# A recurrent memory-attention branch rebuilt around token-stationary column tiles, a list-scheduled order and precomputed tokens

One core of a Trainium2 chip (trn2). The metric is the device time of one execution in microseconds (us).

## The reference, cut to what matters

```python
# A: sliding-window attention over 2048 tokens, D = 640, 32 heads of 20, window 256
# B: 64 segments of 32 tokens, one after the other; 32 heads of 192; 8 memory tokens
mem = mem0
for s in range(64):
    h = concat([mem, x[:, 32*s : 32*s+32]])          # 40 tokens
    q, k, v = h @ Wq, h @ Wk, h @ Wv                 # each 640 x 6144
    p = softmax(where(mask, q k^T * 192**-0.5, -1e9))
    o = (p v) @ Wo                                   # 6144 x 640
    mem = o[:, :8]                                   # the next segment needs this
    outs.append(o[:, 8:])
out = g * A + (1 - g) * B                            # g = sigmoid(x . gate_w)
```

The recurrence makes B a chain of 64 steps. Its four weights are 31.5 MB; both kernels keep a part of them on the chip and load the rest anew in every step.

One caution for all that follows: with these inputs A is of order 1 and B of order 0.001 (its weights carry factors of 640^-0.5 and 6144^-0.5, A's do not). The comparison with the reference hardly sees B.

## The kernel before

```python
def stage_QK(s, g, hT, b, which):                 # 4 groups of 8 heads per step
    ps = ps_mm.tile([P, 512], FP32, name="ps_proj", tag="mm")
    for j in range(TG):                           # 12 column tiles of 128
        for kt in range(KT):                      # 5: D = 5 x 128
            nc.tensor.matmul(ps[:, j*L:(j+1)*L], lhsT=w_tile(which, kt, t), rhs=hT[:, kt, :], ...)   # L = 40
    ...
def stage_V_units(s, g, b, hT):                   # per pair of heads, both of 192
    wvt = wst.tile([P, 1920], BF, name="wv_chunk", tag="w")          # a ring of 5
    nc.sync.dma_start(wvt[:], WvR[i])                                # Wv is streamed whole
    for kt in range(KT):
        nc.tensor.matmul(ps[0:L, ...],    lhsT=hT[:, kt, :], rhs=wv[:, kt, 0:192],   tile_position=(0, 0))
        nc.tensor.matmul(ps[64:64+L, ...], lhsT=hT[:, kt, :], rhs=wv[:, kt, 192:384], tile_position=(0, 64))
...
for k in range(-1, NG + 2):                       # order made by hand: projections of k+1, v of k, output of k-2
    ...
ov = o_ps[:, 0:KT*L]
hT_next = new_hT(s + 1)                           # five small loads, issued late
nc.vector.tensor_copy(hT_next[:, :, 0:M], ov[:, :, 0:M])
```

Wq and Wk are resident, Wv is streamed (16 units of 480 KB per step), Wo in part (4 units).

## Time and profile before

| | before |
|---|---|
| time, median of 2 runs | 3121.92 us (3118.11 to 3125.73) |
| span of the profiled run | 3116.1 us |
| branch A, then the wait for weights | to about 562, to 590 us |
| one step of B | 39.36 us, 64 steps 2519 us |
| array's own work in a step (worked out in the prediction) | 32 us |

Two answers. (The array is TensorE, called PE in the profile; DVE, ACT and POOL are VectorE, ScalarE and GpSimd; "x63" counts instructions.) The first is the view by instruction, cut to one: the cast of the 8 memory tokens into the next step's input, which ends each step; its first and last start give the step, (3067.3 - 626.8)/62. The second is a window of 1600 us inside the loop: busy time of PE, weight load, DVE, ACT, POOL, then granted clock, DMA share and GB/s.

```profile
L587 DVE CAST hT<-ps_o x63: 198/200/201, 626.8 to 3067.3; 128x40 bf16<-128x40 f32 x63
```

```profile
900.00:2500.00 1600.00, 1444.71 (x41309) 1263.49 (x41307) 861.36 (x2037) 438.36 (x1018) 149.27 (x283) 0.98 0.77 257
```

The array is busy 90% of the time.

### The profile page before, as it was taken

What the parts mean: (1) busy time and instruction counts of PE and PEld (TensorE: products, weight loads), DVE (VectorE), ACT (ScalarE), POOL (GpSimd) and SP (SyncE); (2) the same over time, 40 slices, a digit from 0 to 9 for tenths busy, and PEclk for the clock granted to TensorE, in tenths of its full rate; (3) what the DMA queues carried; (4) which work ended last, traced back from release to release, by engine and by line L of the source; (5) the groups of instructions that cost most, each with busy time, mean ns of one, the idle gap of its engine ahead of it and who ended that gap; (6) DMA issues with size and microseconds to landing.
All of it is one profiled execution on the core that took longest, in us unless ns stands there. A gap on an engine that the chain in (4) does not pass through costs nothing.

```text
span 3116.1 us, 155848 instructions
## 1 busy us (share of the span) xinstructions
PE 2739.6 (88%) x71941; PEld 2385.6 (77%) x71957; DVE 1752.1 (56%) x4221; ACT 1102.7 (35%) x2561; POOL 332.2 (11%) x625
## 2 busy tenths in 40 slices
PE   6888888589888889889989999999999998998898
PEld 5777777478777777777777777777788777777777
DVE  5777777355555555555555555555555555555554
ACT  5778787222222222222222222222222222222222
POOL 4300100001000000000000000000000000000000
PEclk9899899799999999999999999999999999999999
DMA  7600000777777777777777777777777777777776
GB/s 256 232 15 15 21 13 8 269 243 265 249 260 250 249 250 257 258 253 254 260 246 257 260 259 259 259 259 262 258 268 261 257 258 250 252 259 253 246 260 219
DMA packets 224367, 699.56 MB, mean 225 GB/s; under 512 B 35416, under 2 KB 50528, under 8 KB 223072
## 3 DMA queue, kind: packets, MB, share of 16 engines
q1 hardware_dynamic: 200624, 646.79, 61.5%
q0 software_dynamic: 22432, 41.98, 4.2%
q8 instruction: 562, 9.21, 1.2%
q10 hardware_dynamic: 656, 0.82, 0.1%
q14 instruction: 93, 0.76, 0.1%
HBM read 671.76 MB, written 17.70 MB: 221 GB/s over the span
## 4 chain that ended last, share of the span: by engine, by line
PE 48%; DVE 19%; DMA 12%; ACT 12%; issue 8%; POOL 1%; SPq 1%; another core or an unknown queue 0%; ACTq 0%; POOLq 0%; DVEq 0%
PE ps_proj L414 14%; DMA wv_chunk<-WvR 9%; PE ps_v L477 8%; PE ps_o L521 7%; PE S_ps L433 4%; ACT a_ex L194 3%; PE PT_ps L457 3%; PE ps_pv L496 3%; DVE sm_sum L449 3%; DVE sm_mx L444 3%; ACT sm_ex L447 3%; ACT a_pt L204 2%; ACT OTg L500 2%; DVE Vp L482 2%; DVE Pg_12543 L452 2%
## 5 line engine op out<-in xcount | busy, mean ns | idle before, releaser
L477 PE MATMUL ps_v<-wv_chunk,hT 128*40 128x192 bf16 x5120 | 615.0, 252 | 61.2 <-DMA wv_chunk<-WvR 58.2
L479 PE MATMUL ps_v<-wv_chunk,hT 128*40 128x192 bf16 x5120 | 616.2, 252 | 2.0 <-issue 2.0
L414 PE MATMUL ps_proj<-hT,Wq_sb 128*128 128x40 bf16 x15360 | 468.0, 181 | 61.1 <-issue 42.2
L414 PEld LDWEIGHTS <-Wq_sb 128*128 128x128 bf16 x15360 | 433.4, 96 | 89.2 <-issue 82.8
L477 PEld LDWEIGHTS <-hT 128*40 128x40 bf16 x5120 | 396.2, 100 | 58.0 <-issue 24.3
L521 PE MATMUL ps_o<-OTg,Wo_res 128*128 128x40 bf16 x11520 | 405.4, 181 | 16.7 <-issue 3.4
L479 PEld LDWEIGHTS <-hT 128*40 128x40 bf16 x5120 | 384.3, 100 | 43.5 <-issue 38.8
L521 PEld LDWEIGHTS <-Wo_res 128*128 128x128 bf16 x11520 | 357.2, 97 | 77.8 <-issue 68.5
L397 POOL DMA_DIRECT2D hT<-xT_dram x320 | 172.2, 545 | 2006.4 <-PE ps_v L479 1966.4
L484 ACT CAST Vp<-ps_v 40x384 bf16<-40x384 f32 x512 | 242.8, 474 | 386.0 <-DVE Vp L482 377.8
L482 DVE CAST Vp<-ps_v 40x384 bf16<-40x384 f32 x512 | 277.8, 543 | 100.6 <-PE ps_v L479 98.6
L194 ACT ACTIVATE a_ex<-s_ps,a_nmx 128x384 bf16<-128x384 f32 (+2 forms) x512 | 289.2, 613 | 75.3 <-DVE a_nmx L192 74.8
L192 DVE TENSOR_REDUCE a_nmx<-s_ps 128x1 f32<-128x384 f32 (+2 forms) x512 | 254.2, 524 | 28.9 <-PE s_ps L189 21.2
L502 DVE CAST OTg<-ps_pv 128x240 bf16<-128x240 f32 x256 | 104.4, 408 | 272.6 <-PE ps_pv L496 272.6
L414 PE MATMUL ps_proj<-hT,Wk_a 128*128 128x40 bf16 x7680 | 235.6, 182 | 20.3 <-issue 20.0
L414 PEld LDWEIGHTS <-Wk_a 128*128 128x128 bf16 x7680 | 217.5, 97 | 32.9 <-issue 32.6
L414 PE MATMUL ps_proj<-hT,Wk_b 128*128 128x40 bf16 x7680 | 236.5, 180 | 5.0 <-issue 4.0
L414 PEld LDWEIGHTS <-Wk_b 128*128 128x128 bf16 x7680 | 216.7, 96 | 16.0 <-issue 15.9
L500 ACT CAST OTg<-ps_pv 128x240 bf16<-128x240 f32 x256 | 91.9, 359 | 353.5 <-PE ps_pv L496 352.0
L420 DVE CAST KTg_12536<-ps_proj 128x480 bf16<-128x480 f32 x128 | 84.2, 658 | 222.8 <-PE ps_proj L414 222.8
L201 PE MATMUL pt_ps<-a_ident,a_ex 128*128 128x128 bf16 x1440 | 161.7, 220 | 42.0 <-ACT a_pt L204 27.4
L449 DVE TENSOR_REDUCE sm_sum<-sm_ex 40x8 f32<-40x320 f32 x256 | 122.3, 478 | 117.3 <-ACT sm_ex L447 113.4
(1165 smaller groups left out, 4481.1 us busy)
## 6 DMA issues: line engine op xcount, KB each, us to landing
wv_chunk<-WvR SPq DMA_DIRECT2D x1024, 480.0 KB, 4.9
wo_chunk<-WoR SPq DMA_DIRECT2D x256, 480.0 KB, 5.2
Wq_sb<-in_B_Wq_dram POOLq DMA_DIRECT2D x5, 1536.0 KB, 13.0
rp_t<-in_B_Wv_dram POOLq DMA_DIRECT2D x16, 480.0 KB, 5.6
WvR<-rp_t POOLq DMA_DIRECT2D x16, 480.0 KB, 4.6
Wo_res<-in_B_Wo_dram SPq DMA_DIRECT2D x12, 480.0 KB, 9.8
hT<-xT_dram POOLq DMA_DIRECT2D x320, 8.0 KB, 5.4
Wk_a<-in_B_Wk_dram POOLq DMA_DIRECT2D x5, 768.0 KB, 8.3
```

Of the source, the lines that this page charges most:

```text
L192: nc.vector.tensor_reduce(out=nmx[:], in_=sp[:, 0:nk * P], axis=AX.X, op=ALU.max, negate=True)
L194: nc.scalar.activation(out=ex[:, 0:nk * P], in_=sp[:, 0:nk * P], func=ACT.Exp, bias=nmx[:], scale=1.0)
L201: nc.tensor.transpose(pt_ps[:, ci, :], ex[:, ci * P:(ci + 1) * P], ident[:])
L397: nc.gpsimd.dma_start(hT[:, kt, M:L], xT_dram[kt, :, s * seg:(s + 1) * seg])
L414: nc.tensor.matmul(ps[:, j * L:(j + 1) * L], lhsT=w_tile(which, kt, t), rhs=hT[:, kt, :], start=(kt == 0), stop=(kt == KT - 1))
L449: nc.vector.tensor_reduce(out=sums[:], in_=ex[:], axis=AX.X, op=ALU.add)
L477: nc.tensor.matmul(ps[0:L, a * 192:(a + 1) * 192], lhsT=hT[:, kt, :], rhs=wv[:, kt, 0:192], start=(kt == 0), stop=(kt == KT - 1), tile_pos ...
L479: nc.tensor.matmul(ps[64:64 + L, a * 192:(a + 1) * 192], lhsT=hT[:, kt, :], rhs=wv[:, kt, 192:384], start=(kt == 0), stop=(kt == KT - 1), ...
L482: nc.vector.tensor_copy(Vp[b][0:L, i0:i0 + npair, 0:192], ps[0:L, 0:npair * 192].rearrange("p (a c) -> p a c", c=192))
L484: nc.scalar.copy(Vp[b][64:64 + L, i0:i0 + npair, 192:384], ps[64:64 + L, 0:npair * 192].rearrange("p (a c) -> p a c", c=192))
L500: nc.scalar.copy(OTg[:, j0:j1, :], src)
L521: nc.tensor.matmul(o_ps[:, dt * L:(dt + 1) * L], lhsT=wsrc[:, jj, dt * P:(dt + 1) * P], rhs=OTg[:, i * 3 + jj, :], start=(t == 0 and dt == ...
```

## The change

The intent: q and k cost 480 matmuls of 40 columns per step, and v fills only 80 of the array's 128 columns (two tiles of 40 tokens). With tokens as the stationary operand, 32 of them fill one of four column tiles, and each quad of matmuls moves 384 columns of four weights at once. To have only 32 tokens (8 of memory and 24 of x) in the loop, the last 8 tokens of each segment, which do not depend on memory, have q, k and v computed once before the loop. q and k come out token-major and are transposed back; values of four heads lie one below the other, so probabilities are expanded to block-diagonal form. A list scheduler written in Python orders the operations of all engines.

```diff
+class Sched:
+    LAT = {"PE": 200, "DVE": 60, "ACT": 60, "POOL": 100, "DMA": 2000}
+    def op(self, eng, dur, fn, reads=(), writes=(), after=()):
+        ...
+        for b in writes:
+            k = b["n"] - self.bufs[b["tag"]]        # buffers of a tag rotate in the order of their making
+            if k >= 0:
+                o["deps"].update(u["n"] for u in self.made[b["tag"]][k]["users"])
...
+    def get(self, ring, kind, pr):                  # Weights: 46 units resident, 18 streamed per step
+        if u in self.tiles:
+            return self.view(kind, self.tiles[u][:])
+        t = ring.tile([P, 1920], BF, name="w_ring", tag="w")
+        self.nc.sync.dma_start(t[:], self.packed[self.slot[u]])
...
+def tail_projections(tc, weights, xTb, xbqk, xbv):  # q, k, v of the last 8 tokens of all 64 segments, to HBM
...
-    wst = ctx.enter_context(tc.tile_pool(name="b_wstream", bufs=5))
+    ring = ctx.enter_context(tc.tile_pool(name="b_ring", bufs=4))
+    ps = {"mm": 3, "tr": 2, "s": 2, "o": 1}         # PSUM banks by use, 8 in all
...
+    def chunk(hT, kind, g):
+        b = sc.buf("mm")
+        def f():
+            ws = [weights.get(ring, kind, 4 * g + j) for j in range(4)]
+            for kt in range(KT):
+                for j in range(4):
+                    nc.tensor.matmul(t[32*j:32*j+32, 0:384], lhsT=tile_of(hT)[:, kt, :], rhs=ws[j][:, kt, :],
+                                     start=(kt == 0), stop=(kt == KT - 1), tile_position=(0, 32 * j))
+        sc.op("PE", 850, f, reads=[hT], writes=[b])  # nothing is said of the ring
...
+    def turn(tok, kind):                            # transposes q or k back
+        b = sc.buf("tr")
...
+        def scores(g):
+            S = sc.buf("s")
+            ...                                     # softmax: 5 DVE operations and one ACT, in place
+            PT = sc.buf("tr")                       # the transposed probabilities share the two transpose banks
+            sc.op("PE", 80, f9, reads=[Pm, Px], writes=[PT])
+            ...                                     # two expansions, f10 and f11
...
+STREAMED = {"q": {0: (3,), 1: (3,), 2: (3,), 3: (3,)}, "k": {0: (2,), 1: (2,), 2: (2,), 3: (2,)},
+            "v": {0: (1, 3), 1: (1,), 2: (1, 3), 3: (1,)}, "o": {0: (3,), 1: (3,), 2: (3,), 3: (3,)}}
```

## The prediction

> **What bounds the kernel now.** I read the page first (busy shares, slices), then every PE instruction of one recurrent step in order of time, then the chain of waits over two steps, then DMA share in short windows.
>
> The page splits the run in two. Slices 0 to 6 are the sliding-window branch (A), where ACT and DVE are busy; slices 7 to 39 are the memory branch (B), where PE is at 8 to 9 tenths and DMA at 7.
>
> ```profile
> PE   6888888589888889889989999999999998998898
> DVE  5777777355555555555555555555555555555554
> ACT  5778787222222222222222222222222222222222
> DMA  7600000777777777777777777777777777777776
> q1 hardware_dynamic: 200624, 646.79, 61.5%
> ```
>
> The memory-token cast into hT closes every step. Its 63 instances start from 626.8 to 3067.3 us, so a step lasts 2440.5/62 = 39.4 us, and 64 steps are 2519 us of the 3116. A ends near 562 us; then PE has almost nothing to do until 590 while weights land. What fills a step is in the groups and the order of time:
>
> ```profile
> L477 PE MATMUL ps_v<-wv_chunk,hT 128*40 128x192 bf16 x5120 | 615.0, 252 | 61.2 <-DMA wv_chunk<-WvR 58.2
> L414 PE MATMUL ps_proj<-hT,Wq_sb 128*128 128x40 bf16 x15360 | 468.0, 181 | 61.1 <-issue 42.2
> L521 PE MATMUL ps_o<-OTg,Wo_res 128*128 128x40 bf16 x11520 | 405.4, 181 | 16.7 <-issue 3.4
> ...
> 1700.20 1.67 PE L414 MATMUL ps_proj<-hT,Wk_a 128*128 128x40 bf16 x60
> 1701.81 0.26 PE L477 MATMUL ps_v<-wv_chunk,hT 128*40 128x192 bf16 x1
> 1701.81 0.26 PE L479 MATMUL ps_v<-wv_chunk,hT 128*40 128x192 bf16 x1
> ...
> 1702.07 0.25 PE L477 MATMUL ps_v<-wv_chunk,hT 128*40 128x192 bf16 x1
> 1702.07 0.25 PE L479 MATMUL ps_v<-wv_chunk,hT 128*40 128x192 bf16 x1
> 1702.15 0.25 PE L477 MATMUL ps_v<-wv_chunk,hT 128*40 128x192 bf16 x1
> 1702.15 0.25 PE L479 MATMUL ps_v<-wv_chunk,hT 128*40 128x192 bf16 x1
> 1702.33 0.42 PE L414 MATMUL ps_proj<-hT,Wq_sb 128*128 128x40 bf16 x10
> ```
>
> The mean of 181 ns is latency, not pitch: 60 projections take 1.67 us, of which 0.18 is the last one's latency, so one per 25.3 ns. The two v matmuls (column tiles 0 and 64) start together, and the next pair 82 ns later. PE's own work in a step is then: q and k 480 x 25.3 ns = 12.1 us, v 80 pairs x 82.5 = 6.6, scores 64 x 25 = 1.6, probability transposes 16 x 58 = 0.9, value products 48 x 26 = 1.2, output projection 240 x 25.5 = 6.1, final transposes 0.3: 28.8 us. Between v's last start and the next projection lie 0.18 us, and 0.12 before v, some 0.1 more on each side than the pitch: 16 v units cost 3.2 us more. So 32 of 39.4 us are PE. The rest shows in the chain: one softmax after another (about 3 us of DVE/ACT hops each), the wait for a streamed weight, and the step's end.
>
> ```profile
> 1703.77 0.49 DVE sm_t_46354 L440
> 1704.28 0.49 DVE sm_mx L444
> 1704.80 0.49 DVE sm_t_46354 L445
> 1705.31 0.48 ACT sm_ex L447
> 1705.82 0.49 DVE sm_sum L449
> 1725.04 4.84 DMA wv_chunk<-WvR
> ```
>
> So PE issue bounds it, with the weight stream close behind: 20 chunks of 491.5 KB per step are 9.83 MB/39.4 us = 250 GB/s.
>
> **What the Trainium skill says.**
> - "TensorE: Matmul & The Clock Gate", Part 1: start-to-start of matmuls does not fall under about 25 ns however few columns move. The trace agrees (25.3 ns at 40 columns, whose streaming would be shorter), so q and k in weight-stationary form pay for issues.
> - The same page, Part 3, packing: matmuls in different column tiles run concurrently, the span being one matmul plus about 4 ns per further tile. With two tiles the trace agrees: 82 ns per pair of 192 columns. No run here has shown four.
> - "TensorEngine Tiling (Array Packing)", Key Properties: a change of tiling mode drains TensorE. The 0.1 us on each side of v agrees.
> - "DMA: Bandwidth & Descriptors", Specifications: line rate needs at least 512 B per transfer. The new store of precomputed q and k has 192 B runs. Nothing here shows that size; the page's list of waits has 10.3 us for the 8 KB store omg_dram in 4 B runs, so small runs are slow to store.
>
> **The change, part by part.**
>
> *PE in a step.* Only 32 tokens (8 memory, 24 new) are projected in the loop. They are the stationary side in four 32-column tiles; 384 weight columns move through each. 12 chunks x 5 contraction tiles = 60 quads, each 384/192 x 82 = 164 ns if four run as two do: 9.8 us in place of 12.1 + 6.6. Transposes back, 24 x 58 = 1.4 (new). Scores: 48 matmuls, 16 x (33 + 25 + 25) = 1.35 against 1.6. Transposes of probabilities 0.3 against 0.9. Block-diagonal values: per group 320 columns once and 160 six times, 133 + 6 x 69 = 0.55 us, 2.2 against 1.2. Output projection 6.1 and final transposes 0.3 stay. Sum 21.5 us. With some 10 to 12 changes into and out of tile mode at 0.2 us: 23.7 us against 32.
>
> *DVE in a step.* Per group: four operations over 320 elements at 0.49 (scale+mask, max, subtract, sum, as in the chain above), reciprocal 0.2, two normalisations 0.42 + 0.22, two block-diagonal expansions over 320 at 0.49, one K eviction 0.3: 4.1, with hops 4.4 us. Four groups are 17.6. It cannot start before the first scores, some 3.6 us into the step (two chunks 1.9, eviction 0.5, transposes 0.4, evictions 0.6), and behind it lie the last value products 0.6, three ACT evictions 1.1, 60 projections 1.6 and the hT cast 0.3. Chain: 3.6 + 17.6 + 3.6 = 24.8 us, if DVE never waits. ACT: 12 token evictions at 0.47, and others, about 16 us: beside it. POOL's small copies and six issues, about 7 us: beside it.
>
> *DMA in a step.* 18 streamed units x 491.5 KB = 8.85 MB instead of 9.83, plus x 0.04, precomputed q/k 0.20 and v 0.10, output and gate 0.08: 9.26 MB. How fast can it go? Three windows:
>
> ```profile
> 1728.00:1731.00 3.00, 2.73 (x84) 2.38 (x81) 2.10 (x6) 0.94 (x2) 0.18 (x1) 1.00 0.93 274
> 1731.00:1734.00 3.00, 2.85 (x100) 2.66 (x97) 1.15 (x4) 0.83 (x2) 2.51 (x5) 1.00 0.97 356
> 1734.00:1737.00 3.00, 2.71 (x94) 2.49 (x91) 1.07 (x2) 0.29 (x1) 0.02 (x1) 1.00 1.05 389
> ```
>
> The last two numbers are DMA share and GB/s: a full queue gives 356 to 389. Over the run the weight queue moved 646.79 MB in 61.5% of 3116 us, 337 GB/s while busy. I take 360: 9.26/0.36 = 25.7 us. So DMA, only two thirds of the step before, becomes the longest of three nearly equal bounds (25.7, 24.8, 23.7). The ring also shrinks from 5 buffers to 4, with 4.9 us from issue to landing; 18 units by 4 slots are 4.5 cycles per step, each at least 4.9 + 1 us of use, 26.5 us. Three balanced bounds on in-order queues do not overlap fully; I add about 1.5 us and choose 27.5 us per step, 64 x 27.5 = 1760 us in place of 2519. The step's start gains: x for the next step is one prefetched transfer, not five issued late.
>
> *Before the loop.* A keeps its work; five small stores per block give way to POOL copies and one store: no change, 562 us. Then 22 resident units (10.8 MB) load while PE waits, about 30 us as now (362 GB/s in that stretch). New is the precomputation: q and k are 960 matmuls of 256 columns at 109 ns (2.4 columns per ns, as in the v pairs, plus 2.5) = 105 us, v 320 x 162 = 52 us: 157 us, bare new PE time. Its 16 stores of 4096 runs of 192 B are 256 runs per engine; at an estimated 20 ns they take 5 us, under the 6.5 us of matmuls they lie beside. I take 165 us, and 10 us for constants and the first loads of B.
>
> Sum: 562 + 30 + 165 + 10 + 1760 + 7 (last output) + 6 (measured time less span, 3121.9 - 3116.1) = 2540 us. The loop gains 759 us and the precomputation gives back some 165.
>
> **The rivals.**
> 1. *PE bound, everything else hidden.* The list-scheduled order hides softmax and DMA; a step is about 24.3 us, the run 2335. For: x is prefetched, DMA reached 389 GB/s. Against: the weight wait is already 20% of the chain in the two steps I read, with 5 buffers and a DMA share of 0.77.
> 2. *Starved ring or serial softmax.* DMA at 337 GB/s gives 27.5 us alone; with the dependence of each step's first projection on the last output projection on top, 31 us per step and 2765 in all. For: QT, K02, Kz and the expanded probabilities have one buffer each.
> 3. *Stores of short runs bound the precomputation.* From the omg store I estimate (10.3 - 2)/128 = 65 ns per run: 256 x 65 = 16.6 us per store, 266 us in place of 105. The run would be 2700. For: the skill's 512 B. Against: 256 B runs of xT land in 1.8 us.
> 4. *Four column tiles do not run together* (300 ns per quad): 60 x 0.14 = 8 us more per step, almost the whole gain, 2900 to 3000. Against: two tiles show no loss, and 8 instructions per 164 ns are 20 ns each, slower than the 13 ns that the 40-column stream keeps.
>
> **Range and chances.** 1 sets the low end, 2 and 3 the high end; 3 and 2 together are rare. Range 2340 to 2760. Even the fourth would be faster by over 2%, so only a combination or a blunder (a store that stalls, a cold clock) could spoil it: 0.96 faster, 0.03 same, 0.01 slower.
>
> **What would show it.** In the changed profile: casts into hT 27.5 us apart (24 says rival 1, 31 rival 2); quads 164 ns apart; DMA share about 0.9 to 0.95 in the loop at 335 to 345 GB/s, and waits of the chunk matmuls for w_ring in the chain; DVE near 18 us per step; the stretch from the last A work to the first loop chunk about 205 us, PE busy in all but 30 to 40 of it. A DMA share under 0.8 with a chain of softmax lines would say that DVE's order, not the stream, set the step. Stores of precomputed q/k that take over 7 us each would say rival 3.

## More of the kernel before

Where I call a kernel's results right, this rests on its edit changing only where a value is kept or when it is computed, and on the race and memory checks.

## The result, and the profile after

The changed kernel takes 3421.17 us (3420.35 to 3421.99, 2 runs), 1.095 times the time before, 95% interval 1.091 to 1.099. The prediction of 2540 us was wrong in sign. Ratios here and below are the mean time of one kernel's fast runs over that of the other's of the same rounds, so not quite the ratio of the medians.

The page's slices of the changed kernel:

```profile
PE   6988886887777777777777777777777777777776
DVE  6777773323333333333434433333433334343333
PEclk9989898898888888878889888878888888888887
DMA  8100004966667666666677666766666666666665
```

The loop starts in slice 9 (counted from 0). There no engine is full: the array, DVE and DMA all have room, and the granted clock, at 9 to 10 tenths before, is at 8. The same two answers as before:

```profile
L755 DVE CAST t_hT<-ps_o x63: 198/200/201, 814.6 to 3371.4; 128x40 bf16<-128x40 f32 x63
```

```profile
900.00:2500.00 1600.00, 1192.00 (x23164) 801.17 (x23153) 635.95 (x1635) 587.74 (x1593) 255.55 (x857) 0.83 0.69 227
```

A step is (3371.4 - 814.6)/62 = 41.24 us, where I had said 27.5 and before had 39.36. The loop costs 64 x 1.88 = 120 us more than before. It also begins later: the first loop matmul starts at 772.5 us instead of 590, 183 us for the precomputation. The sum, 303 us, accounts for the measured difference of 299. To break even a step would have to be at most 36.5 us (39.36 less 183/64).

What stops the array? Three groups of the page, with the idle time before them and who ended it:

```profile
L556 PE MATMUL ps_v<-w_ring,t_hT 128*32 128x384 bf16 x1920 | 327.5, 359 | 187.9 <-DMA w_ring<-w_packed 187.7
L675 PE MATMUL PT_ps<-ident,b_Pm 128*128 128x40 bf16 x512 | 55.3, 186 | 224.5 <-DVE b_Pm L661 224.5
L702 PE MATMUL ps_pv<-t_PTx,b_xv 128*128 128x320 bf16 x256 | 90.7, 354 | 148.5 <-DVE t_PTx L686 148.2
```

With the smaller groups (40.2 us before the streamed output weights, 30.5 before the scores, 18.7 before q) the array waits 234/64 = 3.7 us per step for the ring and 6.6 us for softmax and evictions. In the remaining 31 us it is busy, longer than the 23.7 that the work was worth. In order of time, the array's instructions of one group, with waits in brackets:

```profile
2020.31 0.53 PE L556 MATMUL ps_q<-w_q,t_hT 128*32 128x384 bf16 x3
...
2022.95 0.22 PE L675 MATMUL PT_ps<-ident,b_Pm 128*128 128x40 bf16 x2 [2.10 <-DVE b_Pm L661]
2023.08 0.19 PE L677 MATMUL PT_ps<-ident,b_Px 128*128 128x40 bf16 x1
2023.12 0.33 PE L569 MATMUL tr_k<-ident,t_tok 128*128 128x128 bf16 x3
2024.25 0.30 PE L702 MATMUL ps_pv<-t_PTx,b_xv 128*128 128x320 bf16 x1 [0.81 <-DVE t_PTx L686]
...
2025.12 0.27 PE L624 MATMUL S_ps<-b_Kz,b_QT 128*128 128x80 bf16 x1
```

The k transpose of the next group (`tr_k`) stands right behind the probability transposes of this one (`PT_ps`), which wait for its whole softmax; so the next scores come only after it, and the two score banks never work for two groups. DVE shows this: the first operation of a softmax (L634, into `S_ps`) and the one that writes its probabilities (L661, into `b_Pm`), above in the changed kernel, below in e1, where the rotation is gone:

```profile
2018.84 0.49 DVE L634 SCALAR_TENSOR_TENSOR S_ps<-S_ps,bmask 40x320 f32<-40x320 f32 x1 [4.11 <-PE S_ps L627]
...
2022.47 0.42 DVE L661 TENSOR_TENSOR b_Pm<-S_ps,sm_rs 40x256 bf16<-40x256 f32 x1
...
2025.90 0.49 DVE L634 SCALAR_TENSOR_TENSOR S_ps<-S_ps,bmask 40x320 f32<-40x320 f32 x1 [1.50 <-PE S_ps L627]
```

```profile
2029.27 0.49 DVE L634 SCALAR_TENSOR_TENSOR S_ps<-S_ps,bmask 40x320 f32<-40x320 f32 x1 [2.84 <-PE S_ps L627]
...
2031.17 0.49 DVE L634 SCALAR_TENSOR_TENSOR S_ps<-S_ps,bmask 40x320 f32<-40x320 f32 x1 [0.30 <-PE S_ps L627]
...
2032.89 0.41 DVE L661 TENSOR_TENSOR b_Pm<-S_ps,sm_rs 40x256 bf16<-40x256 f32 x1
```

Between 1000 and 1600 us the two kinds alternate strictly over 58 softmaxes of the changed kernel, so none starts before the probabilities of the one before are written; in e1 they come in pairs, two starts and then two ends. Part of this is written in the scheduler. In its model the two transpose banks rotate through q transpose, k transpose and probabilities (and once per step the final transposes), so the k transpose of group g+1 must wait for the last expansion of group g. Its own plan, which the program can print without a chip, is 34.7 us per step. I had not followed that rotation.

The other delay, in the chain of waits:

```profile
2010.96 0.85 PE ps_k L556 x20
2011.82 5.12 DMA w_ring<-w_packed
2016.98 1.18 PE ps_v L556 x17
2018.16 0.18 PE S_ps L624
```

The first q and k groups use up the four prefetched units; v asks for two more, and the first scores of the step, which need nothing of v, stand behind it in the queue. The scheduler put v there to fill time and knew nothing of the ring.

The third is the clock. The same quad of q matmuls at two moments:

```profile
2012.26 0.34 PE L556 MATMUL ps_q<-w_q,t_hT 128*32 128x384 bf16 x3
...
2012.43 0.33 PE L556 MATMUL ps_q<-w_q,t_hT 128*32 128x384 bf16 x3
...
2019.06 0.51 PE L556 MATMUL ps_q<-w_q,t_hT 128*32 128x384 bf16 x3
...
2019.35 0.53 PE L556 MATMUL ps_q<-w_q,t_hT 128*32 128x384 bf16 x3
...
2019.67 0.53 PE L556 MATMUL ps_q<-w_q,t_hT 128*32 128x384 bf16 x3
```

165 ns apart in the first case (mean of the five quads), as predicted for four tiles that run together; 320 in the second. Windows of 3 us (columns as above) show when:

```profile
2003.00:2006.00 3.00, 1.15 (x9) 0.93 (x10) 1.76 (x6) 0.02 (x1) 0.00 (x0) 0.66 0.58 191
2006.00:2009.00 3.00, 2.74 (x64) 2.34 (x61) 0.04 (x1) 0.98 (x3) 0.53 (x1) 0.50 0.08 20
...
2015.00:2018.00 3.00, 1.36 (x19) 0.55 (x18) 0.00 (x0) 0.29 (x2) 0.00 (x0) 0.94 0.99 329
2018.00:2021.00 3.00, 2.85 (x36) 1.38 (x35) 1.46 (x3) 1.06 (x3) 0.85 (x4) 0.50 0.84 288
```

In both pairs a window in which the array works less than half the time is followed by one at clock 0.50. This is a tendency, not a rule: cut into 534 such windows from 900 us on, the loop has 96 with the array busy less than 1.5 us, and the window after them has a mean clock of 0.585 (0.55 or less in 58 of them, 0.95 or more in 6); after the 174 with 2.7 us or more it is 0.943. The first pair is a softmax wait, with DMA at 20 GB/s since the ring is full; the second is a ring wait, with DMA full. So softmax and ring take turns in stopping the array, and after such waits the work behind them tends to run slower. "TensorE: Matmul & The Clock Gate" of the Trainium skill (Part 1, the two states) describes exactly these two clocks, half for an idle array and full for a busy one, and the windows at 0.50 and 1.00 agree. I had read it and put no term for it in the sum, because before the change the clock was 0.98.

### The profile page after: what moved, and what is told of

Same layout as the page of the kernel before. It is cut to its first block, busy times and chain, and to the rows that moved or that the text cites. A ratio compares the mean times of both kernels' runs of the same rounds, so it can differ in the third digit from the quotient of the medians.

```text
span 3420.3 us, 107679 instructions
## 1 busy us (share of the span) xinstructions
PE 2606.8 (76%) x46613; PEld 1845.1 (54%) x46613; DVE 1498.6 (44%) x3834; ACT 1427.6 (42%) x3713; POOL 511.3 (15%) x1616
## 4 chain that ended last, share of the span: by engine, by line
PE 46%; DMA 21%; DVE 15%; ACT 11%; issue 5%; SPq 1%; POOL 0%; ACTq 0%; DVEq 0%; POOLq 0%
DMA w_ring<-w_packed 19%; PE ps_q L556 8%; PE ps_o L736 7%; PE ps_k L556 6%; PE ps_v L556 5%; ACT a_ex L195 3%; PE t_psum L416 3%; PE S_ps L624 2%; DVE t_PTx L686 2%; ACT a_pt L205 2%; DVE sm_sum L649 2%; ACT b_Kz L602 2%; DVE b_Pm L661 2%; PE ps_pv L702 1%; DVE t_PTm L682 1%
## 5 line engine op out<-in xcount | busy, mean ns | idle before, releaser
L556 PEld LDWEIGHTS <-t_hT 128*32 128x32 bf16 x15360 | 425.2, 107 | 564.5 <-issue 391.4
L556 PE MATMUL ps_v<-w_ring,t_hT 128*32 128x384 bf16 x1920 | 327.5, 359 | 187.9 <-DMA w_ring<-w_packed 187.7
L736 PEld LDWEIGHTS <-w_o 128*128 128x128 bf16 x11520 | 363.5, 100 | 125.9 <-issue 123.2
L736 PE MATMUL ps_o<-t_OT,w_o 128*128 128x40 bf16 x11520 | 400.4, 186 | 16.5 <-ACT t_OT L718 2.3
L634 DVE SCALAR_TENSOR_TENSOR S_ps<-S_ps,bmask 40x320 f32<-40x320 f32 x256 | 125.9, 492 | 535.1 <-PE S_ps L627 535.1
L556 PE MATMUL ps_q<-w_q,t_hT 128*32 128x384 bf16 x3840 | 328.0, 396 | 18.7 <-DVE t_hT L755 18.4
L556 PE MATMUL ps_v<-w_v,t_hT 128*32 128x384 bf16 x3200 | 331.5, 359 | 0.0
L556 PE MATMUL ps_q<-w_ring,t_hT 128*32 128x384 bf16 x1280 | 322.3, 395 | 5.7 <-DMA w_ring<-w_packed 5.5
L556 PE MATMUL ps_k<-w_k,t_hT 128*32 128x384 bf16 x3840 | 303.5, 373 | 0.0
L556 PE MATMUL ps_k<-w_ring,t_hT 128*32 128x384 bf16 x1280 | 299.9, 373 | 0.5 <-DMA w_ring<-w_packed 0.5
L602 ACT COPY b_Kz<-tr_k 64x128 bf16<-64x128 bf16 x512 | 132.7, 259 | 384.8 <-DVE t_K L598 372.5
```

The source lines that it names most:

```text
L556: nc.tensor.matmul(t[32 * j:32 * j + 32, 0:384], lhsT=tile_of(hT)[:, kt, :], rhs=ws[j][:, kt, :], start=(kt == 0), stop=(kt == KT - 1), ti ...
L602: nc.scalar.copy(tile_of(Kz)[64 * r:64 * r + 64, :, r, 0:SEG], src)
L634: nc.vector.scalar_tensor_tensor(out=view(), in0=view(), scalar=scale, in1=mask[:].unsqueeze(1).to_broadcast([L, 8, L]), op0=ALU.mult, op1 ...
L736: nc.tensor.matmul(t[:, dt * L:(dt + 1) * L], lhsT=w[:, b, dt * P:(dt + 1) * P], rhs=OT["tile"][:, 3 * i + b, :], start=(g == 0 and i == 0 ...
```

## The experiments

Theory S: softmax chains are serialised by bank rotation and order. Theory R: ring and stream. Theory C: the half clock is a cause of its own. A step is measured by the cast into hT, as above; clock and GB/s are of 900 to 2500 us. Where "busy" or "waits" per step are given, they are the array's in the same window.

| kernel | time, us (median) | ratio to before | us per step | clock | GB/s |
|---|---|---|---|---|---|
| before | 3121.92 | 1 | 39.36 | 0.98 | 257 |
| changed | 3421.17 | 1.095 | 41.24 | 0.83 | 227 |
| e1_pt_in_score_bank | 3208.98 | 1.027 | 37.73 | 0.89 | 248 |
| e2_no_stream (wrong) | 3070.08 | 0.982 | 35.90 | 0.85 | 14 |
| e3_both (wrong) | 2743.64 | 0.878 | 30.74 | 0.94 | 16 |
| e4_warm | 3260.60 | 1.043 | 38.85 | 0.97 | 240 |
| e5_ring8 (wrong) | 2797.29 | 0.895 | 31.65 | 0.93 | 295 |
| e6_banks | 3152.95 | 1.009 | 37.01 | 0.91 | 253 |
| e7_banks_ringaware | 2817.17 | 0.904 | 31.78 | 0.99 | 296 |
| e8_program_order | 4964.54 | 1.588 | 65.55 | 0.69 | 143 |
| e9_ringaware_only | 3196.70 | 1.023 | 37.83 | 0.87 | 248 |
| e10_e7_no_stream (wrong) | 2561.33 | 0.819 | 27.91 | 1.00 | 18 |
| e11_even_stream | 2701.05 | 0.866 | 30.08 | 0.98 | 311 |
| e12_ring5 | 2598.61 | 0.833 | 28.66 | 0.99 | 326 |

**e1_pt_in_score_bank.** A score tile is declared with 512 columns and scores take 320; the transposed probabilities fit behind them.

```diff
-            PT = sc.buf("tr")
+            pt = lambda: S["tile"][:, 8 * L:11 * L].rearrange("p (a l) -> p a l", l=L)
-            sc.op("PE", 80, f9, reads=[Pm, Px], writes=[PT])
+            sc.op("PE", 80, f9, reads=[Pm, Px], writes=[S])
```

> The changed kernel with one part altered: the transposed probabilities go into the unused columns 320 to 440 of their own score bank, so that the two transpose banks no longer rotate through them and the k transpose of group g+1 need not wait for the last expansion of group g. Right results. Theory S (the four softmax chains of a step run one behind the other because of that rotation, and this costs most of the time): the plan that the program's own scheduler makes falls from 34.7 to 32.3 us per step, and the measured step from 41.2 to 36 to 39 us, the run 3200 to 3330 us. Theory R (the weight stream through a ring of 4 buffers sets the step): at most 1 us per step, above 3350 us. Theory C (the array's half clock after idle stretches sets it): a little less idle time, granted clock a little over 0.84, 3250 to 3400 us.

3.5 us per step, 212 us. This is in S's range, outside R's, and below C's (3250 to 3400 us). But the clock rose with it, from 0.83 to 0.89: of the 3.5 us, 1.5 are fewer waits and 2.0 shorter busy time of the array (30.7 to 28.7 us), so e1 alone does not refuse that the clock costs too. The step also stays far above the plan's 32.3 us.

**e2_no_stream.** In the loop a streamed unit is read from the resident unit before it.

```diff
+        if self.alias:
+            return self.view(kind, self.tiles[kind, pr - 1][:])
         t = ring.tile([P, 1920], BF, name="w_ring", tag="w")
```

> Wrong results on purpose: in the loop every streamed weight unit is read from a resident unit instead, so no weight transfer is left in the loop; everything else, the order too, is as in the changed kernel. Theory R (ring and stream set the step): the step falls from 41.2 to 27 to 30 us, the run to 2500 to 2700 us. Theory S (serial softmax by buffers and order): the step falls only to what the scheduler's own plan says without transfers, 34.7 us, 34 to 36.5, the run 2960 to 3120 us. Theory C: if the waits for weights are what lets the clock fall, the granted clock in the loop rises from 0.83 to 0.95 or more here; if it stays at 0.83 to 0.88 the idle time of the softmax alone is enough to keep it low.

35.9 us: S's figure, near the scheduler's plan of 34.7. With no weight transfer at all the changed kernel still is not within 8 us of my prediction. So the stream, which I had taken for the longest bound, is not what keeps the step above 35.9 us. C: the clock rises only to 0.85, so the waits that are left, mostly for DVE, are enough to keep it low.

**e3_both.** The two edits together.

> Wrong results on purpose: no weight transfers in the loop, as in the run without stream, and the transposed probabilities in the score bank. Theory S: the plan's 32.3 us per step or up to 1.5 us over it, the run 2850 to 2950 us, and granted clock above that of the run without stream alone. Theory R: no better than the run without stream alone.

30.7 us, and 2744 us in all, below S's range (32.3 us and more, 2850 to 2950 us); R is refused. The edits save 3.5 and 5.3 us alone and 10.5 together, 1.7 more than their sum. That each stop hides behind the other and that the clock, 0.94 now, gives back the rest is argued, not separated.

```profile
900.00:2500.00 1600.00, 1341.94 (x31088) 965.49 (x31085) 787.37 (x2185) 792.79 (x2136) 342.67 (x1145) 0.94 0.06 16
```

**e4_warm.** Idle matmuls fill the array's waits for DVE.

```diff
+                for _ in range(5):
+                    nc.tensor.matmul(t_[:, 128:512], lhsT=ident[:], rhs=weights.tiles["q", 0][:, 0:384], start=True, stop=True)
                 # then the probability transposes; likewise 6 of 192 columns ahead of the value products
```

> Right results, extra work: the changed kernel with five idle matmuls of 384 columns ahead of each transpose of probabilities and six of 192 columns ahead of each group of value products, 1.28 us of array time per group at full clock, 5.1 us per step, into unused columns. They fill time in which the array waits for DVE (4.9 us per step by the profile after). Theory C: granted clock in the loop rises from 0.83 to over 0.92, the doubled duration of the other matmuls goes away, and the step falls by 2 to 5 us in spite of the added work, the run 3100 to 3290 us. Against C: the clock stays under 0.88, or it rises and the time does not fall (3400 us and more), since the chain is made of DVE and transfer waits.

```profile
900.00:2500.00 1600.00, 1335.66 (x26323) 913.50 (x26327) 670.19 (x1728) 616.58 (x1686) 270.17 (x904) 0.97 0.72 240
```

The clock goes to 0.97 and the step falls by 2.4 us, although 5.1 us of array work (at full clock) were added to it. C holds: the half clock costs at least 2.4 us per step of its own. It goes with the waits, though: below, where these shrink, the clock is back at 0.99.

**e5_ring8.** Eight ring buffers on top of e1; four resident units of the output projection are read from their neighbours to make room.

```diff
-    ring = ctx.enter_context(tc.tile_pool(name="b_ring", bufs=4))
+    ring = ctx.enter_context(tc.tile_pool(name="b_ring", bufs=8))
```

> Wrong results on purpose: the kernel with the probabilities in the score bank (3209 us), with a ring of 8 weight buffers instead of 4; room for it is made by reading four resident output-projection units from their neighbours, so the 18 transfers per step stay. Without transfers that kernel took 30.7 us per step, with them 37.7. Theory depth (4 buffers are too few: the loop's order asks for several units in a burst and the queue stands idle with a full ring at other times): with 8 the step falls by 4 to 6.5 us to 31 to 34, the run 2780 to 2960 us, and the mean rate rises from 248 to over 275 GB/s. Theory rate (the transfers' speed binds): at most 1.5 us per step, above 3110 us.

```profile
900.00:2500.00 1600.00, 1332.77 (x30163) 945.04 (x30163) 766.06 (x2126) 765.24 (x2072) 333.04 (x1111) 0.93 0.85 295
```

6.1 us per step less, the same 18 transfers, and only 0.9 us more than without any (e3). Depth, not rate: the same DMA now carries 295 instead of 248 GB/s, and the array's ring waits go from 4.1 us per step to none. Four buffers did not let it work ahead while the array waited for softmax. Of the 6.1 us, 2.4 are shorter busy time at the higher clock.

**e6_banks.** On top of e1, the transpose bank that it frees becomes a fourth matmul bank.

```diff
-    ps = {"mm": 3, "tr": 2, "s": 2, "o": 1}
+    ps = {"mm": 4, "tr": 1, "s": 2, "o": 1}
```

> Right results: the kernel with the probabilities in the score bank, and the one transpose bank so freed given to the matmul outputs (four matmul banks, one transpose bank, instead of three and two). The program's own plan falls from 32.3 to 30.2 us per step. Theory S (buffers and order serialise): step 35.0 to 36.5 instead of 37.7, run 3020 to 3130 us. Theory ring depth: below 0.8 us per step of gain, above 3150 us, as the weight waits take what the banks give.

0.7 us: the lower expectation, that of a ring which takes what the banks give. The ring waits rise from 4.1 to 4.7 us per step.

**e7_banks_ringaware.** e6, and the scheduler models the ring; a second edit, not shown, drops its 200 ns hop from matmul to matmul.

```diff
+        def landing(i):                      # when the i-th streamed unit is there
+            while len(land) <= i:
+                k = len(land)
+                t = land[-1] + 1450 if land else 0
+                if k >= 4:
+                    t = max(t, rel[k - 4] + 3700)
+                land.append(t)
+            return land[i]
+        def start(o):
+            t = at[o["n"]]
+            return max(t, landing(len(rel) + o["w"] - 1)) if o["w"] else t
-                t0 = max(free.get(eng, 0), min(at[o["n"]] for o in rs))
+                t0 = max(free.get(eng, 0), min(start(o) for o in rs))
+            rel += [t0 + o["dur"] + 200] * o["w"]
```

> Right results: as the kernel with four matmul banks, and the list scheduler knows of the ring: a matmul group that reads streamed units may start only when the unit would have landed (estimates from the traces: 1.45 us between landings, 3.7 us from the release of a buffer), and matmul after matmul on the same engine costs no hop. Its plan is 29.7 us per step with the transfers in it. If it is the blindness of the order to transfers that costs (theory order), the step falls to 31 to 34 us, the run 2770 to 2960 us. If the depth of the ring itself costs, whatever the order, it stays above 34.5 us, 3000 us.

```profile
900.00:2500.00 1600.00, 1330.69 (x30151) 923.11 (x30151) 773.12 (x2114) 755.97 (x2069) 333.73 (x1108) 0.99 0.88 296
```

5.2 us per step, without any buffer more: the new order does about what four more buffers did in e5. Ring waits fall from 4.7 to 2.9 us, other waits by 1.2, and the array's busy time by 2.2 at the higher clock. How much the dropped hop did is not separated from the ring model. This kernel already beats the one before by 10%.

**e8_program_order.** The changed kernel without its list-scheduled order.

```diff
-        order.sort(key=lambda x: x[:2])
+        order.sort(key=lambda x: x[2]["n"])
```

> Right results: the changed kernel with one part of the change undone: its operations are issued in the order in which the program lists them, not in the list-scheduled order. All theories expect it slower, since the transposes of probabilities then stand right behind their scores in the array's queue and wait for the whole softmax: 4 groups times about 4 us of idle array more, less what is idle there now, 48 to 58 us per step, the run 3850 to 4500 us. If it is under 3600 us the order buys little and its faults cost little too.

65.5 us, worse than I expected. The list order is worth 24 us per step even with its faults.

**e9_ringaware_only.** The ring model (and no hop between matmuls) in the changed kernel, banks untouched.

> Right results: the changed kernel with only the scheduler's knowledge of the ring (and no hop from matmul to matmul); banks and the rotation of transposed probabilities as in the changed kernel. Its plan is 33.3 us per step. If the order's blindness to transfers is a cause of its own, the step falls from 41.2 to 34.5 to 37 us, the run 2990 to 3160 us, and waits for ring units shrink by half. If the blindness costs only together with the bank rotation, it stays above 38.5 us, 3250 us.

37.8 us, between the two expectations: a gain of 3.4, less than the range. And the expected mechanism is not what happened. Per step the array's ring waits stay at 3.7 us; its waits for the probabilities fall from 3.5 to 1.3 us, presumably since the new order has other work ready there. So this gain is not shown to come from knowing the ring. The larger gain of e7 over e6 comes only when the bank rotation is gone.

**e10_e7_no_stream.** e7 without weight transfers, as in e2.

> Wrong results on purpose: the ring-aware kernel with four matmul banks (2817 us, 31.8 us per step), with all streamed units read from residents. What remains of the transfers' cost there: if its 2.8 us per step of array waits for ring units are all of it, 28.5 to 30 us per step, the run 2610 to 2710 us; if transfers cost nothing any more, above 31 us, 2770 us.

27.9 us, below the range that I gave. Transfers still cost e7 3.9 us per step, more than the array's 2.9 us of ring waits.

```profile
900.00:2500.00 1600.00, 1415.60 (x34273) 1011.34 (x34265) 869.75 (x2405) 849.46 (x2349) 378.08 (x1261) 1.00 0.07 18
```

That this is close to the predicted 27.5 us is partly luck: it has no stream, for which the prediction had a chain of 24.8 us. At clock 1.00 the array is busy 24.7 us of the step; in the changed kernel the same work keeps it busy 30.7.

**e11_even_stream.** e7 with the streamed units spread evenly, and later estimates (1500 and 4200 ns).

```diff
-            "v": {0: (1, 3), 1: (1,), 2: (1, 3), 3: (1,)}, "o": {0: (3,), 1: (3,), 2: (3,), 3: (3,)}}
+            "v": {0: (1,), 1: (1,), 2: (1,), 3: (1,)}, "o": {0: (3,), 1: (1, 3), 2: (1, 3), 3: (3,)}}
```

> Right results: the ring-aware kernel with the same 18 streamed units per step spread more evenly (value units 1, 1, 1, 1 instead of 2, 1, 2, 1; two more of the output projection streamed), and later estimates in the scheduler (1.5 us between landings, 4.2 us from release). Its plan falls from 29.7 to 28.3 us. If bursts are what is left of the ring's cost, step 30 to 31.2 us, the run 2700 to 2790 us; if the rate of transfers binds (9.26 MB per step were 291 GB/s at 31.8 us), no gain, 2800 to 2850 us.

1.7 us, the size expected if bursts were part of what was left. The estimates changed with it, so the two are not told apart.

**e12_ring5.** e11 with a fifth buffer; room comes from writing the output in place over its gate tile. The scheduler's estimates changed slightly with it.

```diff
-    ring = ctx.enter_context(tc.tile_pool(name="b_ring", bufs=4))
+    ring = ctx.enter_context(tc.tile_pool(name="b_ring", bufs=5))
-            nc.vector.scalar_tensor_tensor(out=tile_of(res)[:], in0=ox["tile"][0:SEG]...
+            nc.vector.scalar_tensor_tensor(out=ga["tile"][:], in0=ox["tile"][0:SEG]...
```

> Right results: the kernel with the evenly spread stream (2701 us, 30.1 us per step), with a fifth ring buffer, for which room is made by combining the output in place in its gate tile and by letting the initial memory use that tile too; the scheduler knows of five buffers (1.45 us between landings, 4.5 us from release; its plan stays 28.3 us). If the ring's depth still costs, step 28.5 to 29.6 us, the run 2600 to 2675 us. If the rate of the transfers binds by now (DMA share 0.91 and 311 GB/s at 30.1 us), step above 29.7 us, 2680 us and more.

```profile
900.00:2500.00 1600.00, 1424.24 (x33282) 1000.83 (x33280) 855.82 (x2335) 816.99 (x2286) 367.62 (x1227) 0.99 0.93 326
```

28.7 us per step, 2598.61 us, 0.833 of the time before (0.829 to 0.837), 24% under the change as it was given. This refuses the second expectation, that the rate binds above 29.7 us. DMA share is 0.93, but the array waits only 0.4 us per step for the ring and is busy 25.5: its own work is the largest part again. How far the stream is from its own limit no run shows.

## Why the prediction was wrong, point by point

1. *Array work of 23.7 us per step, with four column tiles running as two do:* held. Quads are 165 ns apart at full clock (predicted 164), and without transfers at clock 1.00 (e10) the array is busy 24.7 us per step. Rival 4 is refused.
2. *Before the loop, 205 us from A's end at 562:* the sum held (the first loop matmul starts at 772.5 us, 210), its parts by luck. The array stood still for 30.7 us, about the 30 predicted, but in the middle of the q matmuls: the first store of q was issued only at 605.9 us, behind the resident weights' loads in SP's queue. The 192 B stores landed in 7.0 us (median), with the array never waiting in 86 us of q and k work: rival 3 (16.6 us a store, 2700 us; my sign was "over 7 us each") is refused, if not by much, since the DMA share was 0.87 or more in every 20 us of it. v took 74 us instead of 52: its evictions waited 82 us in sum for the 96 KB v stores, runs of 384 B, to which the prediction gave no time. The allowances of 8 and 10 us about cover that.
3. *"Chain: 3.6 + 17.6 + 3.6 = 24.8 us, if DVE never waits":* this step failed. Its durations were right (a DVE operation over 320 elements took 0.48 to 0.49 us), its condition was not: DVE is busy 636 of 1600 us, 16.4 of 41.2 us per step. Cut at the casts (means of 23 steps from 1000 to 2000 us): the first softmax starts 9.9 us after the cast, where the prediction had the first scores at 3.6 (its own four terms give 3.4); the fourth starts 23.0 us after the first, where it had 3 x 4.4 = 13.2; the rest takes 8.3, where it had 4.4 + 3.6 = 8.0. The four groups run one behind another because of the transpose banks' rotation and the array's order, and the first of them behind v. In e12 the three parts are 7.3, 13.0 and 8.4 us: the middle one is then as predicted, the first still is not, and why is open. I named single buffers as a sign for rival 2 but looked at QT, K02 and Kz, and did not follow the one tag that the transposes and the probabilities share. My sign "a DMA share under 0.8 with a chain of softmax lines" came true (0.69), but the chain also held the ring. e1 removes part of it (3.5 us), e7 with e6's banks most; in e9 the softmaxes still run strictly one behind another, so its 3.4 us come from elsewhere.
4. *"18 units by 4 slots are 4.5 cycles per step, each at least 4.9 + 1 us":* too smooth. It needs a ring that always works. In the changed kernel it is full during softmax and empty in bursts; e5 (depth, 6.1 us) shows it; e7 over e6 (order, with the hop, 5.2 us) and e11 (spread, with estimates, 1.7 us) agree. Whether the limit itself, about 26 us, is right no run shows: e12 does not contradict it at 28.7.
5. *"I add about 1.5 us" for imperfect overlap:* the mis-sized term: over the longest of the three bounds, 25.7, the step has 15.5 us more. (Nor does the sum close: 25.7 + 1.5 is 27.2 and 26.5 + 1.5 is 28.0, not 27.5.) Three nearly equal bounds on engines that wait for one another are a warning, not a small correction.
6. *The clock:* no term for it at all. At a mean of 0.83 the array lost 0.17 x 41.2 = 7 us per step of clock, partly in time when it was idle anyway; the same work kept it busy 6.0 us longer than in e10 (30.7 against 24.7), and e4 shows at least 2.4 us on the path. Rival 2 (31 us) named the right mechanism, a serial softmax or a starved ring, without this, and added a quarter of what was missing (3.5 of 13.7 us).

The gain was therefore not absent from the structure. It was turned into waits: 41.2 us became 37.7 (bank), 37.0 (fourth bank), 31.8 (new order), 30.1 (even spread) and 28.7 (fifth buffer).

## What to carry to other kernels

When a change takes the array off the critical path, sum up what then orders the work: list every buffer tag with all kinds of tile that rotate through it, and read the array's queue as the order in which things will wait (here the first scores behind v's weights), before trusting a sum of bounds. A generated order is only as good as the resources it knows of; a stream that it leaves out turns up as a stall in front of unrelated work. And losses from waiting compound: in the changed kernel the clock was 0.585 in the mean after a window of 3 us in which the array had waited more than half the time.

## What the Trainium skill lacked or had wrong

- "TensorE: Matmul & The Clock Gate", Why this matters for your kernels: it asks for no idle gap of more than about 3 us between bursts. Here the clock fell to 0.50 where the longest single waits shown were 1.48 and 0.98 us (at 2003.87 and 2005.20 us), in a window with the array busy 1.15 of 3 us. Only short gaps that added up went before that fall. (The page's section on a second failure mode does tell of frequent short idling, without a length.)
- The same page, Part 3: it gives a measured speed-up of 2.38 for three column tiles of 32 and none for four alone. In a stream of quads of 384 columns four tiles kept 165 ns per quad, no slower than the two-tile stream before (82 ns per 192 columns).
- "DMA: Bandwidth & Descriptors", Specifications: it gives 512 B as the least for line rate, and the page has no measured rate of trn2 stores to HBM below it. 768 KB in runs of 192 B landed in 7.0 us (median of 16), beside 86 us of q and k matmuls that they did not hold up.
